# Soft-MoE combine weights laid out by PE and ACT, a second inner-layer buffer, dispatch maxima read from PSUM

## The chip, the cores and the metric

The kernel runs on one core of a Trainium2 chip. The metric is the device time of one execution in microseconds (us), as the median of several runs. Engines are named as the profiler names them: PE (matrix products; PEld is its weight load), DVE (VectorE), ACT (ScalarE), POOL (GpSimd) and SP, which here issues DMA transfers. Each engine executes its own instructions in program order and waits on semaphores for the others.

## What is computed

Three layers follow one another. Pooled attention has 8 batches of 8 heads with 576 queries of width 64, and keys and values averaged over groups of 8. Its 4608 output rows of width 512 are the tokens x of a soft mixture of experts, with 8 experts of 4 slots each. Then comes a two-layer network of inner width 2048.

```python
# attention, per batch and head
attn = softmax(q @ mean8(k).T / 8)
x = (attn @ mean8(v))              # -> 4608 x 512
# soft mixture of experts
logits = x @ phi                   # 4608 x 32
d = softmax(logits, axis=0)        # dispatch, over the tokens
slot_input = (d.T @ x).reshape(8, 4, 512)
for e in range(8):
    h = np.maximum(slot_input[e] @ w1[e], 0.0)   # 512 x 1024
    slot_out[e] = h @ w2[e]                      # 1024 x 512
c = softmax(logits, axis=1)        # combine, over the 32 slots
y = c @ slot_out.reshape(32, 512)
# network
r = np.maximum(y @ w_in, 0.0)      # 512 x 2048
out = (s * (r * r) + b) @ w_out    # 2048 x 512
```

## The kernel before

**Attention and dispatch.** A hand-written order of steps (the tables `LOOP` and `FIRST`) goes over the batches, two batches to a pair `pr`, and over their token tiles of 128. PE's short products share a ring of four PSUM banks (tile name `w`, handed out by `bank()`). When a batch's logits are there, its dispatch runs as a generator whose `yield`s are slots of the loop: column maxima (L546, L555), spread to all partitions by a product (L558), copied out of PSUM into `m_all` (L559, DVE), subtracted from the logits (L562, DVE), exponential (L564, ACT), then products of the result with the attention weights (L586, L591). Each batch uses its own maxima, and at the end the eight are brought to one scale (L524 to L534), which needs the copies in `m_all`.

**Experts.** The 8 MB of `w1` and as many of `w2` arrive in 32 transfers of 1 MB in the order of the list `EORD`, numbered n0 to n31 here. Experts 0 to 3 are group 0, experts 4 to 7 group 1. n0 to n7 are group 0's `w1`, n8 and n9 the first two of group 1's, n10 to n15 the first six of group 0's `w2`, n16 to n21 the other six of group 1's `w1`, n22 and n23 the last of group 0's `w2`, n24 to n31 all of group 1's. For a `w1` key PE runs four products (L969) into two PSUM tiles `l1[g]`, for a `w2` key four products (L977) into `so_ps`. The profile counts each of these as two matmuls. When a group's `w1` keys are done, `hidden(g)` copies the two PSUM tiles to `si_all` (L946 on ACT, L947 on DVE), turns them round by products with a selector (`hps`, L951) and writes the relu of that into `h1z` (L953, ACT), a zero-filled buffer with four columns per expert from which the `w2` products read their stationary operand. There is one `h1z`, for both groups. Loads come by SP's queue: `done(key)`, behind a key's products in the program, gives the slot back, and `pump()` puts the next load (L140) into SP's queue, where it waits for those products.

**Between the keys.** `BEHIND` says after which key which side work is started. `step_convs()` moves generators on that rewrite the network's weights to rounded high and low parts (L829 to L843 on DVE, ACT and POOL). Their DVE steps, ten at a time, stand in DVE's queue in front of L947.

**Combine weights.** The combine softmax (L748 to L758) leaves its weights in `L_all`, tokens on the partitions, 4 batch pairs of 32 slots beside one another, 9 token tiles per pair. The network's first product needs `cT`: slots on the partitions, tokens along the row, the rounded value (hi) in the 32-row blocks 0 and 2 and the remainder (lo) in blocks 1 and 3. `combine_t`, begun behind n15, transposes nine tiles on PE (L926), rounds them on ACT back into `L_all` (L927), forms the remainder on DVE in `kept[3]` (L929), a weight slot that is free by then, and then has SP move the bytes with 16 transfers of 32 partitions, 144 KB each (L935), into the four blocks of `cT`, pair after pair. SP's queue issues in program order, so the loads of the network's weights that come after stand behind these 16.

**Hand-over.** After n31 two products (L1004) on the `cT` data fill time on PE, `so_ps` is copied (L1008), turned round by products (L1011), copied (L1014), multiplied with `w_in` (L862, L868, L879, L884) to the matrix `S`, and `st_h` takes `S` with `cT` to the network's inner layer (L1050), of which relu, square and rounding follow (L1054 to L1079). The products L1106 with `w_out` then fill PE to the end.

## Time and profile before

| what | us |
|---|---|
| median of 3 runs (lowest, highest) | 693.62 (692.23, 693.72) |
| the profiled execution's own time | 692.57 |
| its span, first to last instruction | 690.8 |
| PE busy | 649.7 (94%) |
| DVE busy | 475.8 (69%) |
| ACT busy | 399.9 (58%) |
| POOL busy | 287.1 (42%) |
| matmuls of L1106 | 659.9 (225.2 + 224.9 + 209.8) |

The profile is of one execution; its times are from the start of the span. The three groups of L1106 overlap one another in PE's pipeline, so their sum is more than the time they take. The page's share of PE is a mean over stages with different limits. The stages, as the trace has them: attention to 203.2, the experts to 245.4, the hand-over to 251.6, the network from there to about 683, and the last output transfers. A view by windows gives the busy time of each engine in a stretch, and the granted clock of PE (1.00 is 2.4 GHz, 0.5 is 1.2 GHz). The timeline of an engine lists its instructions in order, runs of the same instruction put together (xcount), with the idle time in front and what ended it. The chain goes back from the last instruction to what released each step. An instruction of SP with a `DMA_DIRECT2D` is an issue; its landing is much later.

### The profile page before, as it was taken

Reading aid. Unit: us, or ns where it says so; the run is one execution under the profiler, and the core shown is the slowest. Engines: PE = TensorE matmul, PEld = TensorE weight load, DVE = VectorE, ACT = ScalarE, POOL = GpSimd, SP = SyncE. Lnnn points to the kernel's source line nnn. Section 1 sums busy time; section 2 is a strip of 40 time slices with the busy share of each in tenths; the row PEclk is TensorE's granted clock in tenths of the full one; section 3 lists DMA queues with packets and bytes.
Section 4 is the critical chain, followed back from the end, with each engine's and each line's share of the span. In section 5 each row is a group of like instructions: output and inputs, shape, how many; then the busy total and the mean of one; then the engine's idle time right before and its main releaser. Section 6 shows DMA issues by size and latency. Waiting matters only on the chain.

```text
span 690.8 us, 11197 instructions
## 1 busy us (share of the span) xinstructions
PE 649.7 (94%) x4307; PEld 520.0 (75%) x4307; DVE 475.8 (69%) x748; ACT 399.9 (58%) x659; POOL 287.1 (42%) x220
## 2 busy tenths in 40 slices
PE   7877989799989889999999999999999999999996
PEld 6665777678653358888888888888888888888885
DVE  6879778767663947887677778887556764566443
ACT  3565667566421267886666666666666666555551
POOL 3766466522100443563223434443232241899200
PEclk9998999999679899999999999999999999999999
DMA  8999486607599992011110110301100000222222
GB/s 287 399 340 288 154 245 245 218 29 258 185 362 374 366 277 82 1 61 62 61 62 1 61 62 1 121 14 49 61 1 1 0 1 0 93 93 92 92 92 91
DMA packets 42085, 91.23 MB, mean 132 GB/s; under 512 B 7216, under 2 KB 15408, under 8 KB 42032
## 3 DMA queue, kind: packets, MB, share of 16 engines
q1 hardware_dynamic: 42032, 90.52, 38.4%
q8 instruction: 34, 0.56, 0.3%
q14 instruction: 19, 0.16, 0.1%
HBM read 78.71 MB, written 9.44 MB: 128 GB/s over the span
## 4 chain that ended last, share of the span: by engine, by line
PE 78%; DVE 11%; DMA 4%; ACT 3%; SPq 1%; issue 1%; POOL 0%; DVEq 0%; ACTq 0%
PE o L1106 57%; PE h L1050 5%; PE sc L392 3%; DMA x<-in_moe_w_dram 2%; PE l L969 2%; DVE S L401 2%; DVE mx L399 2%; DVE sm L410 2%; PE w L443 1%; DMA ring<-in_q_dram 1%; PE w L609 1%; ACT S L409 1%; PE w L362 1%; PE w L586 1%; PE w L466 1%
## 5 line engine op out<-in xcount | busy, mean ns | idle before, releaser
L1106 PE MATMUL o<-whi,gh 128*128 128x512 f32 x576 | 225.2, 391 | 1.2 <-ACT gh L1076 1.2
L1106 PE MATMUL o<-wlo,gh 128*128 128x512 f32 x576 | 224.9, 390 | 0.0
L1106 PE MATMUL o<-whi,gl 128*128 128x512 f32 x576 | 209.8, 391 | 0.0
L1079 DVE TENSOR_TENSOR gl<-r,gh 128x768 fp32r<-128x768 f32 (+1 forms) x97 | 104.8, 1081 | 116.4 <-ACT gh L1067 116.1
L1059 ACT ACTIVATE r<-h 128x768 f32<-128x768 f32 x95 | 77.5, 816 | 142.2 <-PE h L1050 140.3
L1106 PEld LDWEIGHTS o<-whi,gl 128*128 128x128 f32 x576 | 108.2, 188 | 22.8
L1106 PEld LDWEIGHTS o<-whi,gh 128*128 128x128 f32 x576 | 108.1, 188 | 21.5 <-ACT gh L1076 1.5
L1106 PEld LDWEIGHTS o<-wlo,gh 128*128 128x128 f32 x576 | 108.2, 188 | 18.9
L842 POOL TENSOR_TENSOR fr<-fr,xp 128x512 f32<-128x512 f32 x28 | 45.2, 1613 | 173.9 <-ACT fr L841 156.7
L1119 DVE SCALAR_TENSOR_TENSOR part<-o,sb_t,part 128x512 f32<-128x512 f32 x144 | 96.9, 742 | 3.2 <-PE o L1106 3.1
L1060 ACT ACTIVATE r<-r 128x768 f32<-128x768 f32 x95 | 80.5, 848 | 3.0
L1067 ACT CAST gh<-r 128x768 fp32r<-128x768 f32 x95 | 79.4, 835 | 2.6
L430 POOL TENSOR_TENSOR P<-S,rs 128x576 f32<-128x576 f32 x32 | 37.3, 1166 | 74.1 <-DVE rs L413 39.1
L1216 POOL TENSOR_TENSOR part<-part,wsum 128x512 f32<-128x512 f32 x36 | 53.3, 1518 | 15.1 <-ACT wsum L1210 15.1
L1050 PE MATMUL h<-cT,S 128*128 128x384 f32 x192 | 49.3, 338 | 0.5 <-DVE S L885 0.5
L1050 PEld LDWEIGHTS h<-cT,S 128*128 128x128 f32 x192 | 36.0, 188 | 8.7 <-DVE S L885 0.7
L410 DVE TENSOR_REDUCE sm<-S 128x8 f32<-128x584 f32 x36 | 27.3, 758 | 20.5 <-ACT S L409 20.4
L392 PE MATMUL sc<-kb,qT 128*128 128x144 f32 x256 | 40.5, 305 | 0.2 <-ACT qT L364 0.2
L399 DVE TENSOR_REDUCE mx<-sc 128x8 f32<-128x576 f32 x36 | 26.4, 733 | 15.6 <-PE sc L392 13.1
L392 PEld LDWEIGHTS sc<-kb,qT 128*128 128x128 f32 x256 | 36.4, 206 | 0.7 <-ACT qT L364 0.5
L409 ACT ACTIVATE S<-S 128x576 f32<-128x576 f32 x36 | 24.6, 682 | 19.4 <-DVE S L401 19.1
L364 ACT COPY qT<-w 128x512 f32<-128x512 f32 x36 | 20.9, 584 | 21.6 <-PE w L362 20.9
(236 smaller groups left out, 884.6 us busy)
## 6 DMA issues: line engine op xcount, KB each, us to landing
x<-in_moe_w_dram SPq DMA_DIRECT2D x15, 1024.0 KB, 9.7
ring<-in_moe_w_dram SPq DMA_DIRECT2D x12, 1024.0 KB, 6.4
raw<-in_moe_w_in_dram SPq DMA_DIRECT2D x8, 1024.0 KB, 5.7
raw<-in_moe_w_out_dram SPq DMA_DIRECT2D x8, 1024.0 KB, 4.8
out_dram<-part SPq DMA_DIRECT2D x32, 256.0 KB, 2.7
ring<-in_q_dram SPq DMA_DIRECT2D x7, 1024.0 KB, 10.8
ring<-in_v_dram SPq DMA_DIRECT2D x9, 768.0 KB, 10.5
ring<-in_k_dram SPq DMA_DIRECT2D x7, 768.0 KB, 8.1
```

The source lines that it names most:

```text
L392: nc.tensor.matmul(out=sc[:, i // 2, 2 * KP * (i % 2):2 * KP * (i % 2) + 2 * KP], lhsT=qT[:, i, :], rhs=kb[:, H * bb + 4 * (j % 2) + i, :] ...
L399: nc.vector.tensor_reduce(out=mx, in_=scv, axis=AX.X, op=ALU.max)
L410: nc.vector.tensor_reduce(out=sm, in_=S, axis=AX.X, op=ALU.add)
L842: nc.gpsimd.tensor_tensor(out=fr, in0=fr, in1=xp, op=ALU.mult)
L1050: nc.tensor.matmul(out=h[x][:, 0:384] if i == 0 else h[:, x, 0:384], lhsT=Sw[:, f, :], rhs=cT(c, 384), start=True, stop=True)
L1059: nc.scalar.activation(out=r, in_=h[:, :, 0:384], func=ACTF.Relu)
L1060: nc.scalar.activation(out=r, in_=r, func=ACTF.Square)
L1067: nc.scalar.copy(out=gh_t[i], in_=r)
L1079: nc.vector.tensor_tensor(out=gl[:, x], in0=r[:, x], in1=gh[:, x].bitcast(F32), op=ALU.subtract)
L1106: nc.tensor.matmul(out=o_t[tt], lhsT=l[:, x, 128 * c:128 * c + 128], rhs=r, start=(fi == 0 and n == 0), stop=(fi == GROUPS[g] - 1 and n == 1),
L1119: nc.vector.scalar_tensor_tensor(out=p, in0=o_t[tt], scalar=sb_t[:, 0:1], in1=p, op0=ALU.mult, op1=ALU.add)
L1216: nc.gpsimd.tensor_tensor(out=p, in0=p, in1=wsum, op=ALU.add)
```

## The change

Three things change.

1. `combine_t` with its transfers goes. In its place `combine_hl(pr)`, one for each pair, forms hi (ACT) and lo (DVE) from the softmax while the tokens are still on the partitions, and puts them side by side, 32 columns each, into `kept[3]`. `combine_t(g)`, six times, transposes three pieces of 128 columns on PE, each with the hi and lo of two token tiles, into one PSUM tile `ct` (two buffers), and ACT copies it into `cT` with four copies of 64 partitions and 384 elements. The new `BEHIND` starts the four `combine_hl` behind n9 to n11 and the six `combine_t` behind n11 to n16. There are 18 transposes for 9, 24 ACT copies and 5 roundings for 3, 5 subtractions for 3, and no transfers for 16.
2. A second `h1z` takes `kept[3]` when the combine is done with it, zeroed on POOL behind n17 (`HZ`). `hidden(1)` writes into it, and its second copy runs on ACT instead of DVE.
3. In the dispatch, the subtraction reads the maxima from PSUM, in the slot where the copy stood; the exponential moves one slot up, and the copy into `m_all` comes after it, one slot later than before.

```diff
--- before.py
+++ after.py
@@ -20,7 +20,8 @@
 WIPOS, WOPOS = 25, 26
 
 
-BEHIND = {15: "c", 18: "i0", 19: "i1", 23: "o0", 24: "o1"}
+HZ = 17
+BEHIND = {9: "c0 c1", 10: "c2", 11: "t0 c3", 12: "t1", 13: "t2", 14: "t3", 15: "t4", 16: "t5", 18: "i0", 19: "i1", 23: "o0", 24: "o1"}
 TAIL = "F0 6 C4 X0 D2 6 X1 E2 6 m 6 6 F2 D3 m D4 6 E4 6 m F4 X2 7 W3 7 W2 7 7 7 M2 6 7 7 M3 6 7 M4 7"
 BUSY = (2, 0)
 CUT = 1
@@ -556,12 +557,12 @@
         yield
         ps = bank()
         nc.tensor.matmul(out=ps[:, 0:32], lhsT=mc.to_broadcast([32, 128]), rhs=ident[0:32, 0:32], start=True, stop=True)
+        dd = ap2.tile([128, 5, 32], F32, tag="dd", name="dd")
+        nc.vector.tensor_tensor(out=dd, in0=Lb, in1=ps[:, 0:32].unsqueeze(1).to_broadcast([128, 5, 32]), op=ALU.subtract)
+        yield
+        nc.scalar.activation(out=dd, in_=dd, func=ACTF.Exp)
         nc.vector.tensor_copy(out=m_all[:, b_, :], in_=ps[:, 0:32])
         yield
-        dd = ap2.tile([128, 5, 32], F32, tag="dd", name="dd")
-        nc.vector.tensor_tensor(out=dd, in0=Lb, in1=m_all[:, b_, :].unsqueeze(1).to_broadcast([128, 5, 32]), op=ALU.subtract)
-        yield
-        nc.scalar.activation(out=dd, in_=dd, func=ACTF.Exp)
         yield
         zd = ap2.tile([128, 32], F32, tag="zd", name="zd")
 
@@ -914,29 +915,34 @@
             convs.append(todo.popleft())
             next(convs[-1])
 
-    def combine_t():
-
-
-        x0 = 0
-        for j0, n in ((0, 4), (4, 4), (8, 1)):
-            x = 128 * n
-            Lc = L_all[:, 1 + j0:1 + j0 + n].rearrange("p j r s -> p (j r s)")
-            ps = ps_x.tile([128, 512], F32, tag="sx", name="ct")
-            for i in range(n):
-                nc.tensor.transpose(out=ps[:, 128 * i:128 * i + 128], in_=Lc[:, 128 * i:128 * i + 128], identity=ident)
-            nc.scalar.copy(out=Lc.bitcast(F32R), in_=ps[:, 0:x])
-            yield
-            nc.vector.tensor_tensor(out=kept[3][:, x0:x0 + x].bitcast(F32R), in0=ps[:, 0:x], in1=Lc, op=ALU.subtract)
-            x0 += x
-        hl = (L_all[:, 1:10].rearrange("p j r s -> p (j r s)"), kept[3][:, 0:x0])
-        for pr in range(NPR):
-            dst = cT(9 * pr * 128, x0).bitcast(F32)
-            for r in range(4):
-                nc.sync.dma_start(out=dst[32 * r:32 * r + 32], in_=hl[r % 2][32 * pr:32 * pr + 32])
+    def combine_hl(pr):
+
+        Lc = L_t[pr][:, 1:10, :]
+        hl = kept[3].rearrange("p (j z s) -> p j z s", z=2, s=32)
+        t0, t1 = 9 * pr, 9 * pr + 9
+        for a, e, o in ((t0, min(t1, 32), t0), (32, t1, 0)):
+            if a < e:
+                z = hl[:, o:o + e - a]
+                x = Lc[:, a - t0:e - t0]
+                nc.scalar.copy(out=z[:, :, 0].bitcast(F32R), in_=x)
+                nc.vector.tensor_tensor(out=z[:, :, 1].bitcast(F32R), in0=x, in1=z[:, :, 0], op=ALU.subtract)
+        yield
+
+    def combine_t(g):
+
+        ps = ps_x.tile([128, 3, 128], F32, tag="sx", name="ct")
+        hl = kept[3].rearrange("p (j x) -> p j x", x=128)
+        for i in range(3):
+            nc.tensor.transpose(out=ps[:, i], in_=hl[:, (3 * g + i) % 16], identity=ident)
+        dst = cT(768 * g, 768).rearrange("p (m a x) -> p m a x", m=3, a=2)
+        for j in range(2):
+            for r in range(2):
+                nc.scalar.copy(out=dst[64 * r:64 * r + 64, :, j], in_=ps[64 * j:64 * j + 64])
+        yield
 
     so_ps = ps_1.tile([128, 512], F32, tag="so", name="so_ps")
 
-    h1z = None
+    h1z = []
     wo_ = [conv_wo(f) for f in range(GROUPS[0])]
     todo.extend(cmb)
     l1 = [[ps_l.tile([128, 512], F32, tag="l1", name="l1") for _ in range(2)] for g in range(2)]
@@ -944,14 +950,14 @@
 
     def hidden(g):
         nc.scalar.copy(out=hs[:, 0:512], in_=l1[g][0])
-        nc.vector.tensor_copy(out=hs[:, 512:1024], in_=l1[g][1])
+        (nc.scalar.copy if g else nc.vector.tensor_copy)(out=hs[:, 512:1024], in_=l1[g][1])
         yield
         hps = ps_1.tile([128, 8, 32], F32, tag="hps", name="hps")
         for fc in range(8):
             nc.tensor.matmul(out=hps[:, fc, :], lhsT=hs[:, 128 * fc:128 * fc + 128], rhs=sel4, start=True, stop=True)
         yield
         nc.scalar.activation(
-            out=h1z.rearrange("p f (e r) -> p f e r", r=36)[:, :, :, 16:20],
+            out=h1z[g].rearrange("p f (e r) -> p f e r", r=36)[:, :, :, 16:20],
             in_=hps[:, :, 4 * EG * g:4 * EG * g + 4 * EG].rearrange("p f (e j) -> p f e j", j=4),
             func=ACTF.Relu,
         )
@@ -976,7 +982,7 @@
             for c in range(4):
                 nc.tensor.matmul(
                     out=so_ps[32 * c:32 * c + 32, :],
-                    lhsT=h1z[:, 4 * hf + c, 36 * ge + 16 - 4 * e:36 * ge + 48 - 4 * e],
+                    lhsT=h1z[g][:, 4 * hf + c, 36 * ge + 16 - 4 * e:36 * ge + 48 - 4 * e],
                     rhs=w[:, c, :],
                     start=(e == 0 and hf == 0), stop=(e == E - 1 and hf == 1),
                 )
@@ -984,16 +990,19 @@
         if n_ == BRIEF:
             brctx.close()
             cT_t.append(ctx.enter_context(tc.tile_pool(name="cv1", bufs=1, side="right")).tile([128, NTH], F32R, name="cT1"))
-        if h1z is None and kept:
-            h1z = kept[0][:, 0:1152].rearrange("p (f r) -> p f r", f=8)
-            nc.gpsimd.memset(h1z, 0.0)
+        if not h1z and kept or n_ == HZ:
+            h1z.append(kept[3 if h1z else 0][:, 0:1152].rearrange("p (f r) -> p f r", f=8))
+            nc.gpsimd.memset(h1z[-1], 0.0)
         advance(hid)
         if key == W1[g][-1]:
             hid.append(hidden(g))
             advance(hid)
-        if n_ in BEHIND:
-            x, f = BEHIND[n_][0], int(BEHIND[n_][1:] or 0)
-            todo.appendleft(conv_wi(f) if x == "i" else islice(wo_[f], 2) if x == "o" else combine_t())
+        for x in BEHIND.get(n_, "").split():
+            f = int(x[1:])
+            if x[0] in "ct":
+                next((combine_hl if x[0] == "c" else combine_t)(f))
+            else:
+                todo.appendleft(conv_wi(f) if x[0] == "i" else islice(wo_[f], 2))
         if key != EORD[-1]:
             step_convs()
     assert not todo, len(todo)
```

PE around the keys n10 to n17, the experts' stage. `so_ps` rows are `w2` keys (n10 to n15), `l_` rows `w1` keys, `ct` the transposes; before:

```order
L977 MATMUL so_ps<-raw_66,ring_76 32x512 x4
L977 MATMUL so_ps<-x,ring_76 32x512 x12
L977 MATMUL so_ps<-ring_81,ring_76 32x512 x4
L977 MATMUL so_ps<-x,ring_76 32x512 x4
L926 MATMUL ct<-ident,L 128x128 x4
L969 MATMUL l_2647<-x,siz 32x512 x2
L969 MATMUL l_2648<-x,siz 32x512 x2
L926 MATMUL ct<-ident,L 128x128 x4
L969 MATMUL l_2647<-x,siz 32x512 x2
L969 MATMUL l_2648<-x,siz 32x512 x2
L926 MATMUL ct<-ident,L 128x128
```

and with the change:

```order
L936 MATMUL ct<-ident,ring_79 128x128 x3
L983 MATMUL so_ps<-x,ring_76 32x512 x4
L936 MATMUL ct<-ident,ring_79 128x128 x3
L983 MATMUL so_ps<-x,ring_76 32x512 x4
L936 MATMUL ct<-ident,ring_79 128x128 x3
L983 MATMUL so_ps<-ring_81,ring_76 32x512 x4
L936 MATMUL ct<-ident,ring_79 128x128 x3
L983 MATMUL so_ps<-x,ring_76 32x512 x4
L936 MATMUL ct<-ident,ring_79 128x128 x3
L975 MATMUL l_2647<-x,siz 32x512 x2
L975 MATMUL l_2648<-x,siz 32x512 x2
L936 MATMUL ct<-ident,ring_79 128x128 x3
```

Three transposes now stand behind each key from n11 to n16, where before all nine stood behind n15, n16 and n17 (before, the row of 12 is three keys).

ACT from `hidden(0)` to `hidden(1)`, in the same stage: L946 and L953 are its copy and relu, L927 the rounding, L841 a conversion of network weights; before:

```order
L946 COPY si_all<-l_2645 128x512
L953 ACTIVATE ring_76<-hps 128x32x4
L927 CAST L<-ct 128x512 x2
L927 CAST L<-ct 128x128
L841 ACTIVATE ring_78<-raw_65 128x512 x2
L946 COPY si_all<-l_2647 128x512
L953 ACTIVATE ring_76<-hps 128x32x4
```

and with the change, where every line number is six higher from `hidden` on and L940 is the copy into `cT`:

```order
L952 COPY si_all<-l_2645 128x512
L959 ACTIVATE ring_76<-hps 128x32x4
L927 CAST ring_79<-L 128x9x32 x3
L940 CAST cT_2629<-ct 64x3x128 x4
L927 CAST ring_79<-L 128x5x32
L927 CAST ring_79<-L 128x4x32
L940 CAST cT_2629<-ct 64x3x128 x8
L940 CAST cT_2704<-ct 64x3x128 x12
L842 ACTIVATE ring_78<-raw_65 128x512 x2
L952 COPY si_all<-l_2647 128x512
L953 COPY si_all<-l_2648 128x512
L959 ACTIVATE ring_79<-hps 128x32x4
```

The 24 copies and the roundings now stand between the two `hidden`s, in front of the conversion and of the two copies L952 and L953.

SP's queue at the end of the experts: `x` is an expert weight slot, `raw_` a slot for raw network weights; before, with the first 2 of the 16 transfers and the last:

```order
L140 DMA ring_81<-in_moe_w_dram 128x4x512
L140 DMA x<-in_moe_w_dram 128x4x512 x2
L935 DMA cT_2629<-L 32x1152
L935 DMA cT_2629<-ring_79 32x1152
...
L935 DMA cT_2704<-ring_79 32x1152
L140 DMA raw_65<-in_moe_w_in_dram 128x4x512
L140 DMA raw_67<-in_moe_w_in_dram 128x4x512
L140 DMA raw_66<-in_moe_w_out_dram 128x2x1024
```

and with the change:

```order
L141 DMA ring_81<-in_moe_w_dram 128x4x512
L141 DMA x<-in_moe_w_dram 128x4x512 x2
L141 DMA raw_65<-in_moe_w_in_dram 128x4x512
L141 DMA raw_67<-in_moe_w_in_dram 128x4x512
L141 DMA raw_66<-in_moe_w_out_dram 128x2x1024
```

The raw loads now follow directly on the last two expert weights.

## Rows read from the trace of the kernel before

**Rows 1.** Windows: busy us (instructions) by engine, granted clock, DMA share, GB/s.

```profile
core 0: us, PE busy (x) PEld busy (x) DVE busy (x) ACT busy (x) POOL busy (x), PEclk, DMA share, GB/s
...
221.00:229.40 8.40, 8.40 (x73) 2.50 (x66) 5.24 (x10) 3.23 (x6) 1.06 (x1) 1.00 1.04 392
229.40:237.40 8.00, 4.88 (x32) 2.97 (x28) 7.76 (x11) 0.35 (x2) 4.13 (x4) 0.67 1.04 386
237.40:245.40 8.00, 7.77 (x64) 1.93 (x64) 4.14 (x5) 1.17 (x3) 5.17 (x4) 0.91 1.03 266
245.40:251.60 6.20, 3.93 (x35) 2.84 (x35) 1.92 (x6) 3.83 (x11) 1.26 (x1) 1.00 0.88 194
```

**Rows 2.** Chain that ended last: start us, us, what.

```profile
221.62 0.59 PE ct L926 x4
...
227.28 16.13 DMA x<-in_moe_w_dram
...
247.31 2.66 DMA cT<-L
```

**Rows 3.** Timeline of PE: start us, us, operation, [idle before <-releaser].

```profile
228.43 1.04 PE L977 MATMUL so_ps<-ring,ring 128*32 128x512 f32 x8
...
233.14 1.92 PE L951 MATMUL hps<-sel,si_all 128*128 128x32 f32 x8 [2.66 <-DVE si_all L947]
234.99 1.94 PE L977 MATMUL so_ps<-ring,ring 128*32 128x512 f32 x8
237.38 1.78 PE L977 MATMUL so_ps<-ring,ring 128*32 128x512 f32 x8 [0.46 <-ACT ring L953]
...
243.28 1.89 PE L977 MATMUL so_ps<-x,ring 128*32 128x512 f32 x16
245.42 0.74 PE L1004 MATMUL l<-cT 128*128 128x512 f32 x2 [0.25 <-DMA cT<-ring]
...
249.48 0.97 PE L1050 MATMUL h<-cT,S 128*128 128x384 f32 x4 [0.46 <-DVE S L885]
```

**Rows 4.** Timeline of DVE, same columns.

```profile
228.48 1.41 DVE L830 TENSOR_SCALAR ring<-ring 128x512 f32<-128x512 f32 x1
...
232.40 0.68 DVE L947 COPY si_all<-l 128x512 f32<-128x512 f32 x1
```

**Rows 5.** Timeline of SP's DMA issues.

```profile
224.28 5.54 SPq L140 DMA_DIRECT2D x<-in_moe_w_dram  x2
229.92 2.53 SPq L935 DMA_DIRECT2D cT<-L  x1
...
249.92 1.23 SPq L140 DMA_DIRECT2D raw<-in_moe_w_in_dram  x2
```

**Rows 6.** DMA view of L140: landings of the issues at 224.28 and 227.28.

```profile
DMA to landing us min/median/max: 14.5/15.3/16.1
```

**Rows 7.** DMA view, 236 to 240 and 240 to 243.4.

```profile
DMA packets 753, 1.55 MB, mean 386 GB/s; under 512 B 32, under 2 KB 32, under 8 KB 753
...
DMA packets 232, 0.68 MB, mean 199 GB/s; under 512 B 69, under 2 KB 69, under 8 KB 232
```

**Rows 8.** Groups of ACT copies by form: busy us, mean ns, idle.

```profile
L282 ACT ACTIVATE kb<-w 64x384 f32<-64x384 f32 x24 | 11.6, 485 | 9.6 <-PE w L275 9.3
...
L323 ACT COPY vpt<-w 64x288 f32<-64x288 f32 x8 | 2.7, 392 | 2.0 <-PE w L316 2.0
```

**Rows 9.** Timeline of ACT, one pair of copies.

```profile
69.03 0.69 ACT L323 COPY vpt<-w 64x288 f32<-64x288 f32 x2
```

**Rows 10.** Timeline of PEld at the last key.

```profile
243.71 0.12 PEld L977 LDWEIGHTS so_ps<-x,ring 128*32 128x32 f32 x4 [0.31 <-DMA x<-in_moe_w_dram]
```

**Rows 11.** Timeline of DVE at the last dispatch.

```profile
195.16 0.19 DVE L559 COPY m_all<-w 128x32 f32<-128x32 f32 x1 [0.50 <-PE w L558]
195.39 0.32 DVE L562 TENSOR_TENSOR dd<-L,m_all 128x160 f32<-128x160 f32 x1
```

**Rows 12.** Waits of PE, whole span: us in total, times, longest.

```profile
PE w L586 <- ACT dd L564: 1.0, 2, 0.8
```

## The prediction

> **What bounds the kernel now.** I read the windows by stage first, then the chain, and then engine by engine the one stage that the change touches. The MLP, from 251.60 us on, is out of reach: its matmuls follow one another without a gap that the change could close. What is left is the stretch between the end of attention (203.2) and the first MLP matmul (251.60): the experts, to 245.4, then the hand-over. In the windows [rows 1] PE is busy for only 4.88 of the 8.00 us from 229.4 to 237.4, at a mean clock of 0.67; from 237.4 to 245.4 it is nearly always busy and the rate of the DMA falls from 386 to 266 GB/s; in the hand-over, 245.4 to 251.6, PE is busy for 3.93 of 6.20.
>
> The printed chain [rows 2] goes through neither PE hole. It goes from the issue of the last expert weight (227.28) over its landing 16.13 us later (243.41), through SP's cT issues to a cT landing at 249.97. I believe its first half and not its second. The PE rows [rows 3] show why: the last two keys (`so_ps` matmuls) run at 243.28 to 245.2, as soon as that weight is there; L1004 then follows at 245.42 with 0.25 us of wait for a cT transfer, and from there a chain of small steps (the `so` copy that began at 245.30, L1011, L862, L868, L879, L884, L1050) reaches L1050 at 249.48. L1050's first half ends at about 249.96, which by itself explains when ACT's relu can start. So **the last weight's landing sets the end of the experts, and the small steps set the hand-over**; the cT transfers take part through what they do to that landing.
>
> PE was late as well. It stood 2.66 us before the second half of `hps`, because L947 on DVE stood behind ten conversion operations of 0.4 to 1.4 us each and ran only at 232.40 [rows 3, 4]. The next matmuls, 233.14 and 234.99, ran 1.92 and 1.94 us per 8, against 1.04 for 8 at 228.43: half clock. Then 0.46 us were lost before 237.38, since the relu into the one `h1z` waits for the readers of group 0. PE reached the last key at about 243.3 to 243.7. **Both limits meet within half a microsecond**, so removing only PE's or only the DMA's delay would give nothing. The change touches both, and the later of the two decides.
>
> **The DMA side.** All 16 cT issues go, 144 KB each: 2.36 MB. Before them the weights land in order and evenly: of the last two, the one issued at 224.28 takes 14.5 us (238.8), the one at 227.28 takes 16.1 (243.4) [rows 5, 6]. So the last one comes 4.6 us after its predecessor. At the steady rate of 386 GB/s 1 MB takes 1.049/0.386 = 2.7 us, and this rate is what holds to 240 [rows 7]. From 240 to 243.4 the same queue completes 232 packets at a mean rate of 199 GB/s. In the windows the engines are as busy as before there [rows 1]; the transfers into 32 partitions are mixed in. Without them the last weight lands at 238.8 + 2.7 = 241.5, **1.9 us earlier**. What now follows in the queue is 1 MB loads of the MLP's weights (before, from 249.92 on [rows 5]); loads of that kind followed one another through the whole stage at the steady rate, so they delay what is ahead of them little: 0 to 0.5 us. The issue of the last two weights must not become late. Their slots come free at keys that end at about 224 to 226 after the change too (below), and they queue for over 14 us, so a delay of 2 us on issue is covered.
>
> **The PE side, replayed.** To 216.3 nothing moves. Then six groups of three transposes stand between the keys n10 to n17, where before 4 + 4 + 1 stood at n15 to n17: nine more. Four take about 0.58 us of PE's time (0.59 in the chain [rows 2]), so nine cost 1.3. Each group is followed by four copies 64x384 out of PSUM on ACT, with two PSUM buffers. Their price has two bounds: 0.485 us each, as L282 (64x384) took [rows 8]; or less where copies overlap, as the 64x288 pair L323, where two of 0.392 took 0.69, so the second came 0.30 after the first [rows 8, 9]. Scaled to 384 elements, 0.30 gives 0.385 (an estimate). A group is then 0.385 x 4 + 0.1 = 1.65 us at the low price, 2.0 at the high one (0.485 x 4 + 0.1). PE has a key (0.97) and three transposes (0.45) per group, 1.4, so ACT paces it: PE waits from the third group on for a buffer. The low price gives about 0.3 to 0.45 at each of three groups, 1.0 in all; the high one about 2.2. I take the low one, since L323 is the same COPY out of 64 partitions of PSUM and L282 is an activation with a scale. The preparation (hi on ACT, the lo subtraction on DVE, for c0 to c3) runs beside the matmuls of n10, in a stretch where both engines waited; only the first group may wait for it, until about 218.0.
>
> So the group-1 keys of `w1`, which ended at 228.6, end at about 228.6 + 1.3 + 1.0 = 230.9 (between 230.2 and 232.1). n22 covers the first copy (L946, 0.59); the second, now on ACT too, ends at about 232.1, so the second half of `hps` starts there and not at 233.14. n23 and then n24 follow without the wait at 237.38, since the second `h1z` is zeroed at n17 and nothing reads it: `hps` ends at 233.1, n23 at 234.1. The holes that are left here are a few tenths each, as those of the hand-over are (0.25 before L1004, 0.46 before L1050 [rows 3]), where the clock stood at 1.00 [rows 1], so I reckon with full clock. Seven keys of 0.97, n24 to n30, end at 234.1 + 6.8 = **240.9**; at the dear copy price 242.1. Before, the half clock and the holes made it about 243.5.
>
> The later of 240.9 and 241.5 + 0.3 (the wait for the weight's load at 243.71 in front of the last key was 0.31 [rows 10]) is 241.8. From the landing to the end of the experts it was 243.4 to 245.2, 1.8, so the end is 243.3: **1.9 us earlier**. The hand-over has the same steps in the same order; L1004's 0.25 us of wait ran beside the `so` copy and gives nothing. The MLP begins 1.9 us earlier and is as long as before, because its weights now come earlier than they did.
>
> ACT's new work is 24 x 0.385 to 0.485, or 9 to 12 us, between 217 and 231; of the 8.4 us from 221 to 229.4 ACT was busy for 3.23 [rows 1]. It delays ACT's conversions (L841) by some five, and with them `ring` operations of DVE and POOL, whose users come in the MLP.
>
> For this choice of engine there is a contrary rule. The rows show 0.485 us for 384 elements on ACT and 0.68 us for DVE's copy of 512 [rows 4, 8]. The Trainium skill, "ScalarE: Activation LUTs", section "Rules for kernel authors", would rather have simple arithmetic on VectorE than on ScalarE. By that rule the six groups would have been split between two engines; here DVE had ten conversions queued at that place, so the sum would gain at most the 1.0 us of buffer waits, which the landing hides.
>
> **The dispatch.** The subtraction no longer waits for the copy of the maxima (0.19) and its gap: at the last batch 195.16 to 195.39, so 0.2 us earlier [rows 11]. In the loop PE waited 1.0 us in two places for that exponential [rows 12], of which half may go. Against it the PSUM bank is held one step longer, for all eight batches; the next users of the four banks can stop. At the batches where I could see a bank's next user close behind, that is 0.15 to 0.5 us each, three of them. Bounds: -1.0 and +1.5; I take -0.1, as both mostly fall beside PE's other work.
>
> **Sum.** 1.9 + 0.1 = 2.0. The profiled execution took 692.57 (span 690.8) and gives 690.6; the median of the runs is 693.62, 1.05 higher, which gives 691.6. I put the forecast between them, and count every case from 693.1: **691.1**.
>
> **The rivals.** *N, the landing stays.* If the last weight's slow stretch has another cause than the cT transfers (it is the last of its kind in the queue), it lands at 243.4 as before and only the dispatch's tenths are left: 692.9. For it: transfers behind another should not delay it, and PE's wait for that weight is but 0.31. Against it: the rate halves just where the cT transfers begin to follow [rows 7], and a single load has no other reason to. The Trainium skill, "DMA: Bandwidth & Descriptors", section "Queues, rings and completion order", says that within one queue of an engine descriptors are taken in ring order. By that alone the cT transfers would cost the weight nothing and the answer would be 692.9; the halved rate in the rows speaks against it, so I leave it 0.13.
>
> *P, ACT paces PE.* If the copies cost 0.485 and c0 to c3 come late, PE reaches the last key at 242.1 or, with waits at all six groups, at 243: the gain is 0.4 to 1.5, so 692.0 to 692.7. Chance 0.10.
>
> *E, both are earlier.* If the landing is at 240 or before and ACT's copies overlap, PE's chain sets the end, 240.9 + 1.0 against 245.2: 3.3, with 0.5 from the dispatch 689.3. Nothing shows a landing before 241, so 0.06.
>
> *T, the other side: half clock in the hand-over.* PE would come to the last key too early, stand for a microsecond or more for the weight, and go on at half clock. In the rows a hole of 2.66 us is followed by 1.92 and 1.94 per 8 matmuls instead of 1.04, and the clock was back only near 239 [rows 3]. The hand-over's PE work on the path is 3.93 - 0.74 (L1004, beside the copy) = 3.2 us [rows 1, 3]; at half clock it is 3.2 longer, against a gain of 2.0: +1.2, so 694.3. It decides if the hole before the last key comes near that one; my replay gives 0.9, and the smaller holes of the hand-over left the clock at 1.00 [rows 1]. Chance 0.09.
>
> *B, the banks.* The longer hold stops PE in attention by 1.5 more than it gains, or slightly above: 692.6 or more. Chance 0.07.
>
> **How the numbers follow.** The forecast has 0.55, N 0.13, P 0.10, E 0.06, T 0.09, B 0.07. A measurement of this kernel can tell about 0.2%, or 1.4 us, from no change. The forecast's gain, 2.0 with some 0.9 to either side, is over 1.4 three times in four: faster 0.41 and same 0.14. With E's 0.06, P and B a little, faster is 0.50; N, P and most of B give same 0.36; T and the rest of B slower 0.14. The range leaves out half of E and much of T: 689.4 to 693.9.
>
> **What would show it.** Right: no `hps` wait on a DVE copy; so_ps at 1.04 per 8 throughout; the last weight 2.7 us behind its predecessor; the experts' end at about 243.3 with the hand-over still 6.2 to 6.4 long. N shows as a spacing of 4.6 without any cT transfer; P as `ct` waits of PE on L940 of over 2 us; T as a clock of 0.5 in L1011 to L1050; B as new PE waits in attention whose releaser is the copy of the maxima.

## The result and the profile after

The changed kernel takes 686.32 us in the median (685.67 to 689.64, 5 executions), the kernel before 693.72 (692.23 to 695.21). The ratio is 0.9903, 95% interval [0.9873, 0.9932]: 6.7 us faster (4.7 to 8.8), against a forecast of 2.0. It lies below the range, which ended at 689.4. The profiled execution took 687.59, its span is 685.8 (before 690.8).

Windows of the changed kernel over the stretches of [rows 1] (columns as there):

```profile
core 0: us, PE busy (x) PEld busy (x) DVE busy (x) ACT busy (x) POOL busy (x), PEclk, DMA share, GB/s
221.00:229.40 8.40, 7.99 (x75) 3.65 (x71) 1.75 (x3) 6.74 (x14) 4.07 (x4) 1.00 1.05 387
229.40:237.40 8.00, 7.64 (x73) 2.11 (x72) 7.75 (x9) 1.58 (x3) 5.21 (x4) 1.00 1.05 386
237.40:245.40 8.00, 6.06 (x44) 4.07 (x37) 2.63 (x7) 4.73 (x12) 4.13 (x4) 0.80 0.66 252
```

From 229.4 to 237.4 PE is now busy for 7.64 us instead of 4.88, at clock 1.00 instead of 0.67, and the DMA keeps 386 GB/s to the last weight. But these windows lie at another place of the program than before: the stage has moved to the left. The timeline of PE (columns as in [rows 3]) shows by how much, first the row of before, then those of after (line numbers up to nine higher):

```profile
203.21 6.07 PE L969 MATMUL l<-ring,siz 128*32 128x512 f32 x32 [0.94 <-DVE siz L631]
```

```profile
197.42 5.54 PE L975 MATMUL l<-ring,siz 128*32 128x512 f32 x32 [0.94 <-DVE siz L632]
...
217.76 0.55 PE L936 MATMUL ct<-ident,ring 128*128 128x128 f32 x3 [0.58 <-ACT cT L940]
...
226.47 1.04 PE L983 MATMUL so_ps<-ring,ring 128*32 128x512 f32 x8
227.48 1.97 PE L957 MATMUL hps<-sel,si_all 128*128 128x32 f32 x16
229.38 1.92 PE L983 MATMUL so_ps<-ring,ring 128*32 128x512 f32 x16
...
236.81 1.07 PE L983 MATMUL so_ps<-x,ring 128*32 128x512 f32 x8 [0.36 <-DMA x<-in_moe_w_dram]
...
242.20 1.62 PE L1059 MATMUL h<-cT,S 128*128 128x384 f32 x4 [0.46 <-DVE S L886]
244.54 0.79 PE L1115 MATMUL o<-whi,gh 128*128 128x512 f32 x1 [0.72 <-ACT gh L1085]
```

The first expert product starts at 197.42; before, it started at 203.21. So **5.8 us are gained before the part of the program on which nearly all of the prediction is spent.** From there to the end of the last key it is 197.42 to 237.9, 40.5 us, against 203.21 to 245.2, 42.0: 1.5 gained. The hand-over takes 237.9 to 244.54, 6.7 against 6.4. The first products of the network then run at half clock to about 249 (0.79 and 0.63 each instead of 0.50 and 0.39), which gives back some 2 us in this execution. 5.8 + 1.5 - 0.3 - 2 is about the 5.0 by which the span shrank.

Where attention gained, two groups of each kernel show (group, busy us, mean ns, idle us before them with its releaser). Before:

```profile
L562 DVE TENSOR_TENSOR dd<-L,m_all 128x160 f32<-128x160 f32 x8 | 6.8, 853 | 0.0
...
L564 ACT ACTIVATE dd<-dd 128x160 f32<-128x160 f32 x8 | 2.7, 336 | 8.8 <-DVE dd L562 8.7
```

and after:

```profile
L561 DVE TENSOR_TENSOR dd<-L,w 128x160 f32<-128x160 f32 x8 | 2.5, 313 | 1.1 <-PE w L559 1.1
...
L563 ACT ACTIVATE dd<-dd 128x160 f32<-128x160 f32 x8 | 2.7, 338 | 2.8 <-DVE dd L561 2.8
```

The subtraction of the maxima took 853 ns in the mean of its eight instructions, and takes 313 now. ACT stood 8.8 us in front of the exponential, with the rest of its queue behind it, and stands 2.8 now. The prediction put no price on it: it counted the copy in front of it at the last batch, where the subtraction's row shows 0.32 us [rows 11]. What made the others slow stands in the timelines of DVE and POOL before, side by side:

```profile
69.50 1.61 DVE L562 TENSOR_TENSOR dd<-L,m_all 128x160 f32<-128x160 f32 x1
...
69.11 1.81 POOL L260 TENSOR_TENSOR ring<-ring 128x768 f32<-128x768 f32 x1
...
90.92 1.86 DVE L562 TENSOR_TENSOR dd<-L,m_all 128x160 f32<-128x160 f32 x1
...
90.80 1.80 POOL L260 TENSOR_TENSOR ring<-ring 128x768 f32<-128x768 f32 x1
```

Each slow subtraction begins just behind a POOL instruction that reads two operands from SBUF, and ends 0.2 us behind that instruction's end (71.11 against 70.92, 92.78 against 92.60; at 113.7 and 133.5 likewise, 1.03 and 1.05 us). With one of its two operands in PSUM it takes 0.31 in all eight batches. The Trainium skill, "SBUF — State Buffer", section "Who interferes with whom", states just this: a DVE instruction with two SBUF inputs contends with a GpSimd instruction that reads SBUF. It calls the port pair that the two share an exclusive lock, and says that a DVE instruction with at most one SBUF input, outside its two-port modes, doesn't contend. The rows agree with it: 1.03 to 1.86 us beside a POOL instruction with two inputs in SBUF, 0.31 with one in PSUM. It would have changed the sum, and the prediction didn't look for it.

### The profile page after: what moved, and what is told of

It reads as the page before. It is cut to its first block, busy times and chain, and to the rows that moved or that the text cites. A ratio compares the mean times of both kernels' runs of the same rounds, so it can differ in the third digit from the quotient of the medians.

```text
span 685.8 us, 11208 instructions
## 1 busy us (share of the span) xinstructions
PE 646.9 (94%) x4316; PEld 516.4 (75%) x4316; DVE 471.0 (69%) x749; ACT 412.6 (60%) x686; POOL 288.3 (42%) x221
## 4 chain that ended last, share of the span: by engine, by line
PE 79%; DVE 10%; DMA 5%; ACT 3%; issue 1%; SPq 1%; DVEq 0%; POOL 0%; ACTq 0%
PE o L1115 57%; PE h L1059 5%; PE sc L393 3%; DVE S L402 2%; DMA x<-in_moe_w_dram 2%; PE w L444 2%; DVE mx L400 1%; DVE sm L411 1%; PE w L363 1%; DMA ring<-in_q_dram 1%; PE w L610 1%; ACT S L410 1%; DMA brief<-in_moe_w_dram 1%; PE w L587 1%; PE w L467 1%
## 5 line engine op out<-in xcount | busy, mean ns | idle before, releaser
L1059 PE MATMUL h<-cT,S 128*128 128x384 f32 x192 | 49.9, 342 | 0.5 <-DVE S L886 0.5
L1059 PEld LDWEIGHTS h<-cT,S 128*128 128x128 f32 x192 | 36.4, 190 | 8.7 <-DVE S L886 0.7
L393 PE MATMUL sc<-kb,qT 128*128 128x144 f32 x256 | 39.0, 297 | 0.2 <-ACT qT L365 0.2
L393 PEld LDWEIGHTS sc<-kb,qT 128*128 128x128 f32 x256 | 35.0, 199 | 0.7 <-ACT qT L365 0.5
```

The costliest lines, as they stand in the source:

```text
L393: nc.tensor.matmul(out=sc[:, i // 2, 2 * KP * (i % 2):2 * KP * (i % 2) + 2 * KP], lhsT=qT[:, i, :], rhs=kb[:, H * bb + 4 * (j % 2) + i, :] ...
L1059: nc.tensor.matmul(out=h[x][:, 0:384] if i == 0 else h[:, x, 0:384], lhsT=Sw[:, f, :], rhs=cT(c, 384), start=True, stop=True)
```

## The experiments

Profiles of one kernel differ by where PE falls to half clock, and times of one kernel's executions by up to 9 us. So each verdict rests on the ratio, and the trace is used for what doesn't hang on the clock.

**The dispatch alone**: the kernel before with the one hunk of the diff that stands in the dispatch.

```diff
+        dd = ap2.tile([128, 5, 32], F32, tag="dd", name="dd")
+        nc.vector.tensor_tensor(out=dd, in0=Lb, in1=ps[:, 0:32].unsqueeze(1).to_broadcast([128, 5, 32]), op=ALU.subtract)
+        yield
+        nc.scalar.activation(out=dd, in_=dd, func=ACTF.Exp)
         nc.vector.tensor_copy(out=m_all[:, b_, :], in_=ps[:, 0:32])
         yield
-        dd = ap2.tile([128, 5, 32], F32, tag="dd", name="dd")
-        nc.vector.tensor_tensor(out=dd, in0=Lb, in1=m_all[:, b_, :]...
-        yield
-        nc.scalar.activation(out=dd, in_=dd, func=ACTF.Exp)
         yield
```

> The kernel before with the third part of the change alone (the subtraction from PSUM one slot earlier, the copy one slot later). In the trace of after, attention ends 5.8 us earlier: 2.1 of it are there at 150 us, the other 3.7 arise between 177 and 195, where PE of before ran at half clock and PE of after did not. Theory D (the dispatch alone makes both): 4 to 6 us faster, about 688.5, and no half clock between 177 and 191. Theory D-: only the 2.1 us come from the dispatch, the clock stretch is a coin that falls anew in each execution: about 691.5. The prediction's own term: 0.1 faster, 693.6.

Ratio 0.9949 [0.9921, 0.9976]: 3.5 us faster (1.7 to 5.5). That lies between theory D and theory D-, and is 35 times the prediction's 0.1. The sign that D named did not come: in this profile the clock from 170 to 190 is 0.83, not 1.00 as in that of the changed kernel. The profile of this kernel also shows what the experts of before do with a gain that comes to them (PE timeline at the last key):

```profile
238.63 1.03 PE L977 MATMUL so_ps<-x,ring 128*32 128x512 f32 x8
241.91 1.07 PE L977 MATMUL so_ps<-x,ring 128*32 128x512 f32 x8 [2.25 <-DMA x<-in_moe_w_dram]
243.80 0.73 PE L1004 MATMUL l<-cT 128*128 128x512 f32 x2 [0.82 <-DMA cT<-ring]
```

PE reaches the last key early and stands 2.25 us for the last weight, then 0.82 more for a cT transfer: the weight still comes late behind its predecessor, and PE, earlier now, can't cover it.

**The rest alone**: the changed kernel with that hunk taken back.

> The changed kernel with the dispatch of before: only the combine by PE and ACT, no transfers, and the second h1z. The prediction's term for this part was 1.9 us: 691.8. If instead most of the measured 7.4 us comes from here (theory X), it is below 689. In its trace the attention part is the same code as before: if the half clock from 177 to 191 is there again, it belongs to that code and is no accident of one execution.

Ratio 0.9960 [0.9934, 0.9985]: 2.8 us faster (1.0 to 4.6), around the 1.9 of the prediction. In its profile the stage from the first expert product (201.70) to the last key's end (241.6) takes 39.9 us, 2.1 less than before, PE waits 0.67 us for the last weight, and L1059 runs at full clock:

```profile
240.49 1.07 PE L983 MATMUL so_ps<-x,ring 128*32 128x512 f32 x8 [0.67 <-DMA x<-in_moe_w_dram]
...
245.86 0.97 PE L1059 MATMUL h<-cT,S 128*128 128x384 f32 x4 [0.46 <-DVE S L886]
```

The two parts together, 0.9949 x 0.9960 = 0.9909, are the whole within the intervals.

**Slot or operand.** Two kernels split the dispatch edit. One moves the subtraction up and leaves both operands in SBUF:

```diff
         nc.vector.tensor_copy(out=m_all[:, b_, :], in_=ps[:, 0:32])
-        yield
         dd = ap2.tile([128, 5, 32], F32, tag="dd", name="dd")
         nc.vector.tensor_tensor(out=dd, in0=Lb, in1=m_all[:, b_, :]...
         yield
         nc.scalar.activation(out=dd, in_=dd, func=ACTF.Exp)
+        yield
```

> The kernel before, copy of the maxima where it was, and behind it in the same slot the subtraction from the copy; the exponential one slot earlier. So the slot moves and the operand does not (both operands in SBUF). Theory O (the operand: a subtraction of two SBUF operands stands while a POOL instruction runs, 1.0 to 1.9 us instead of 0.31 in four batches): the subtraction is still slow wherever POOL runs at its new place, so under 1 us of gain if POOL runs there, the whole 2 us if it does not. Theory S (the slot: only the earlier start matters): the same gain as the dispatch edit as a whole.

The other leaves the slot and changes the operand:

```diff
-        nc.vector.tensor_tensor(out=dd, in0=Lb, in1=m_all[:, b_, :]...
+        nc.vector.tensor_tensor(out=dd, in0=Lb, in1=ps[:, 0:32]...
```

> The kernel before with the copy and the subtraction in their old slots, the subtraction reading the maxima from PSUM. So the operand moves and the slot does not. Theory O: the subtraction takes 0.31 us in all eight batches instead of 0.32 to 1.86, and 1.5 to 2 us of the gain at 150 us are there. Theory S: the subtraction is faster, but the exponential still comes late, and less than 0.7 us of the gain is there.

Ratios 0.9941 [0.991, 0.9973] for the slot, 0.9971 [0.9944, 0.9998] for the operand; the two intervals overlap. The groups of the subtraction and of the exponential, first slot, then operand:

```profile
L561 DVE TENSOR_TENSOR dd<-L,m_all 128x160 f32<-128x160 f32 x8 | 5.5, 692 | 0.3
...
L563 ACT ACTIVATE dd<-dd 128x160 f32<-128x160 f32 x8 | 2.7, 338 | 3.2 <-DVE dd L561 3.1
```

```profile
L562 DVE TENSOR_TENSOR dd<-L,w 128x160 f32<-128x160 f32 x8 | 2.5, 312 | 0.0
...
L564 ACT ACTIVATE dd<-dd 128x160 f32<-128x160 f32 x8 | 2.7, 336 | 5.6 <-DVE dd L562 5.5
```

The stretch from the first L609 of batch 0 to that of batch 1, at full clock in all these profiles, is 19.88 us before (77.75 to 97.63), 18.66 with the slot, 18.62 with the operand and 18.48 after (L610, 77.23 to 95.71). So **in this stretch either half alone brings nearly all of the gain**: each theory got its own kernel right there and was wrong to rule out the other. Whether that holds for the whole time the ratios leave open. With the slot the subtraction is still slow (692 ns), but has a slot of time in hand; with the operand it is fast in the old slot. What cost time there was the exponential's lateness in ACT's queue, by the one exponential that lies in the stretch: ACT waits 1.87 us for its subtraction before and 0.32 with the operand, and with the slot (90.41) and after (87.58) it doesn't wait. First before, then operand:

```profile
92.82 0.34 ACT L564 ACTIVATE dd<-dd 128x160 f32<-128x160 f32 x1 [1.87 <-DVE dd L562]
```

```profile
90.95 0.34 ACT L564 ACTIVATE dd<-dd 128x160 f32<-128x160 f32 x1 [0.32 <-DVE dd L562]
```

That the operand escapes POOL is plain in the timelines of the second one, where the subtraction runs inside a POOL instruction and takes 0.31:

```profile
90.48 1.81 POOL L260 TENSOR_TENSOR ring<-ring 128x768 f32<-128x768 f32 x1
...
90.61 0.31 DVE L562 TENSOR_TENSOR dd<-L,w 128x160 f32<-128x160 f32 x1
```

**The landing of the last weight.** In the kernel before, `combine_t` starts behind n27 instead of n15.

```diff
-BEHIND = {15: "c", 18: "i0", 19: "i1", 23: "o0", 24: "o1"}
+BEHIND = {18: "i0", 19: "i1", 23: "o0", 24: "o1", 27: "c"}
```

> The kernel before with the start of the combine transposes moved from behind n15 to behind n27, so that SP issues three 1 MB loads of the network's weights behind the last expert weight and only then the 16 cT transfers. What is read is the landing of the last expert weight, not the time, which suffers because the network's first product then waits for cT (some 5 us slower than before). If the cT transfers slow the last weight (the prediction's step), it lands 2.6 to 2.9 us behind its predecessor. If it is slow for another reason, being the last (rival N), 4 us or more, as before.

The last two weights are issued at 225.13 and about 2.6 later, and take 14.0 and 14.1 us; the last one lands 2.6 us behind its predecessor, not 4.6 as before. The DMA view over the last one's stretch, and PE's row at the last key:

```profile
DMA packets 504, 1.00 MB, mean 386 GB/s; under 512 B 14, under 2 KB 14, under 8 KB 504
...
241.84 1.06 PE L977 MATMUL so_ps<-x,ring 128*32 128x512 f32 x8 [1.43 <-DMA x<-in_moe_w_dram]
```

386 GB/s, with 1 MB loads behind it in the queue; with cT transfers behind it, 199 [rows 7]. The other profiles say the same: issue and time to landing put the last weight 4.4 to 5.1 us behind its predecessor in all five with cT transfers behind it, and 2.6 to 3.3 us in all seven without. Rival N falls, and with it the time that the prediction worked out from the ring order. The Trainium skill, "DMA: Bandwidth & Descriptors", section "Queues, rings and completion order", speaks of the order in which descriptors are taken, which no run here shows; whatever it was, the transfers behind did slow the load ahead. (The time, 705.25 in one execution, is of no use: the network waits for cT.)

**PE's hole alone.** The kernel before with the second copy of `hidden(1)` on ACT.

```diff
-        nc.vector.tensor_copy(out=hs[:, 512:1024], in_=l1[g][1])
+        (nc.scalar.copy if g else nc.vector.tensor_copy)(out=hs[:, 512:1024], in_=l1[g][1])
```

> The kernel before with one thing of the second part alone: the second copy of group 1 on ACT instead of DVE. The prediction says that PE's delay and the last weight's landing meet within half a microsecond, so that removing PE's alone gives nothing: PE's hole of 2.66 us and the half clock behind it go, PE waits 2 us or more for the last weight instead, and the time is within 0.7 us of before. Theory X: PE's hole was the bound, and 2 us or more are gained.

Ratio 1.0027 [1.0004, 1.005]: 1.9 us **slower** (0.3 to 3.5). The hole of 2.66 in front of `hps` is gone, and PE's rows read:

```profile
227.98 1.97 PE L951 MATMUL hps<-sel,si_all 128*128 128x32 f32 x16
...
237.98 1.06 PE L977 MATMUL so_ps<-x,ring 128*32 128x512 f32 x8 [1.22 <-DMA x<-in_moe_w_dram]
242.38 1.35 PE L977 MATMUL so_ps<-x,ring 128*32 128x512 f32 x8 [3.34 <-DMA x<-in_moe_w_dram]
...
247.49 1.08 PE L862 MATMUL o<-ring,sot 128*32 128x128 f32 x16 [0.45 <-ACT sot L1014]
...
250.05 1.65 PE L1050 MATMUL h<-cT,S 128*128 128x384 f32 x4 [0.26 <-DVE S L885]
```

PE now stands 1.22 and 3.34 us for the last two weights, and the products behind that run at half clock (L862 1.08 instead of 0.65, L1050 1.65 instead of 0.97). That is rival T as it was drawn, with the wait that it needs. From the first expert product (201.85) to the last key's end this profile takes 41.9 us, as before (42.0), and the hand-over takes 8.7 instead of 6.4. So in this pair of profiles the experts gained nothing, and the loss is in the hand-over's clock. The DMA's half shortens the wait and doesn't rule the fall out: in the six profiles of the changed kernel and its variants PE waits for that weight 0, 0, 0.36, 0.67, 0.88 and 1.87 us, and the first products of the network run at half clock in three of them: at 0.36, at 1.87 and at 0 (the last one of the runs below).

**One buffer.** The changed kernel with a single `h1z`.

```diff
-        if not h1z and kept or n_ == HZ:
+        if not h1z and kept:
...
-            out=h1z[g].rearrange("p f (e r) -> p f e r", r=36)[:, :, :, 16:20],
+            out=h1z[0].rearrange("p f (e r) -> p f e r", r=36)[:, :, :, 16:20],
...
-                    lhsT=h1z[g][:, 4 * hf + c, 36 * ge + 16 - 4 * e:36 * ge + 48 - 4 * e],
+                    lhsT=h1z[0][:, 4 * hf + c, 36 * ge + 16 - 4 * e:36 * ge + 48 - 4 * e],
```

> The changed kernel without its second h1z buffer: the relu of group 1 waits again for the readers of group 0 and the last keys read the one buffer. Prediction's step: the second buffer saves a wait of 0.46 us of PE, and the last weight's landing decides, so within 0.7 us of the changed kernel. Theory C (the wait matters because PE's clock falls after it): 2 us or more slower, with half clock behind n23.

Ratio 0.9901 [0.9867, 0.9936] beside 0.9905 for the changed kernel on the same chip: no difference that can be measured. The wait is there (0.40 on ACT's relu) and the last weight hides it. In this profile too the hand-over fell to half clock behind a wait for the weight:

```profile
229.97 1.07 PE L983 MATMUL so_ps<-ring,ring 128*32 128x512 f32 x8 [0.40 <-ACT ring L959]
...
238.06 1.07 PE L983 MATMUL so_ps<-x,ring 128*32 128x512 f32 x8 [1.87 <-DMA x<-in_moe_w_dram]
...
243.74 1.65 PE L1059 MATMUL h<-cT,S 128*128 128x384 f32 x4 [0.26 <-DVE S L886]
```

**The changed kernel once more**, with no edit.

> The changed kernel once more, beside the others. Its ratio, measured 0.9903, against the sum of its two parts measured alone (0.9949 and 0.9960, together 0.9909). Additive parts: 0.988 to 0.993. If the dispatch's gain is lost in the experts of before, where the last weight then waits for the DMA (the profile of the dispatch alone shows PE waiting 2.25 us for it), the whole is more than the sum: below 0.989. In the profile, the clock from 170 to 200 and from 242 to 250 tells whether the half clock seen there belongs to the code.

Ratio 0.9905 [0.987, 0.994]: the first figure stands, and it is as near to the product of the parts as the intervals can tell. In this profile L1059 (243.60, 0.98) and what follows ran at full clock, so the half clock at the start of the network belongs to single executions. No wait stands in front of the last key here: PE, and not the weight, was the later of the two. From 170 to 190 the clock is 0.83 in this profile and 1.00 in the first, so that stretch too differs between executions of one kernel.

**Filling the hand-over.**

```diff
-OPS = "o0 a0 o0 a1 b0 b1 h0 g0 o1 h1 o1 g1"
+OPS = "o0 a0 o0 a1 b0 b1 h0 w2 g0 o1 h1 o1 g1"
-BUSY = (2, 0)
+BUSY = (2, 1)
```

> The changed kernel with three more filler products in the hand-over: one behind L1020 and two behind the first L1059. In the profile of the changed kernel PE runs at half clock from L1059 at 242.2 to about 249, some 2 us lost. If the holes of the hand-over bring that on (theory C), the filled version runs L1059 and the first L1115 at full clock and is 0.5 to 2 us faster in the median. If the fall has nothing to do with these holes, the same time, or 0.3 us slower for the added products.

Ratio 0.9896 [0.9861, 0.9932] against 0.9905: inconclusive. The hand-over was at clock 1.00 in this profile, but so it was in the unfilled one above.

**Filling the end of attention** (`W` and a number in `TAIL` are so many transposes of the identity).

```diff
-TAIL = "F0 6 C4 X0 D2 6 X1 E2 6 m 6 6 F2 D3 m D4 6 E4 6 m F4 X2 7 W3 7 W2 7 7 7 M2 6 7 7 M3 6 7 M4 7"
+TAIL = "F0 6 C4 X0 D2 W8 6 X1 E2 6 m 6 6 F2 D3 m D4 6 E4 6 m F4 X2 7 W3 7 W2 7 7 7 M2 6 7 7 M3 6 7 M4 W5 7 W5"
```

> The changed kernel with idle products of PE (transposes of the identity, 128x128) in three holes at the end of attention: eight in the hole of 1.6 us before L554, five in that of 0.92 before the last L620, five in that of 0.94 before the first expert product. In all profiles so far PE runs at half clock for one, two or three stretches of about 6.8 us between 170 and 210, and the times of one kernel's executions follow the mean clock. Theory C (these holes bring the stretches on): the clock is 1.00 to 210 and the time 2 to 4 us below the changed kernel, about 683 to 685. Theory C- (the stretches come from something else): no difference, or up to 1 us slower for the added products.

Ratio 0.9901 [0.9876, 0.9926], as the changed kernel. The clock rose as theory C says, up to a point (its mean over an execution is 0.985 to 0.988 in the six executions here, 0.975 to 0.985 in the eleven of the changed kernel), but its 2 to 4 us did not come: the time stayed. Windows (columns as in [rows 1]) of the kernel before, of the changed one and of this one:

```profile
170.00:190.00 20.00, 18.34 (x161) 14.14 (x162) 13.52 (x29) 8.78 (x24) 4.60 (x4) 0.69 0.50 173
190.00:210.00 20.00, 17.59 (x187) 10.36 (x179) 14.20 (x45) 4.70 (x13) 1.61 (x2) 0.80 0.97 358
```

```profile
170.00:190.00 20.00, 16.55 (x214) 11.95 (x216) 15.18 (x37) 9.17 (x27) 4.42 (x4) 1.00 0.71 253
190.00:210.00 20.00, 17.45 (x158) 9.18 (x156) 12.96 (x39) 3.65 (x9) 1.06 (x1) 0.83 1.02 374
```

```profile
170.00:190.00 20.00, 17.34 (x218) 13.10 (x210) 14.71 (x36) 8.23 (x24) 4.43 (x4) 1.00 0.71 253
...
190.00:196.80 6.80, 6.70 (x88) 6.04 (x81) 4.24 (x16) 1.18 (x4) 0.00 (x0) 1.00 1.01 406
...
203.50:210.50 7.00, 6.93 (x40) 1.62 (x40) 2.41 (x9) 0.46 (x2) 0.00 (x0) 0.57 1.04 388
...
203.56 1.94 PE L975 MATMUL l<-brief,siz 128*32 128x512 f32 x8 [3.13 <-DMA brief<-in_moe_w_dram]
```

Here PE is at full clock until it begins the experts at 196.79; then it stands 3.13 us for the weight in `brief`, and behind that its mean clock is 0.57. In this profile what the clock gives, the landing of that weight takes back (the first profile of the changed kernel waited 0.69 us for it, at 203.65, and the second not at all). No version of these beats the changed kernel by more than the intervals.

## Why the prediction was wrong

**The step that failed is the dispatch term.** "Bounds: -1.0 and +1.5; I take -0.1": measured alone it is 3.5 us (1.7 to 5.5), outside its own bounds. Three readings made it small. It counted the copy of the maxima and its gap, 0.2 us at the last batch [rows 11], and put the subtraction's own length at nothing gained: that batch's row has 0.32 us for it, where the group has a mean of 853 ns. It counted only PE's wait for the exponential, 1.0 us [rows 12], where ACT waited 8.8 us for the subtraction and what stands behind it in ACT's queue came late: at 72.45 PE waited 1.05 us for a copy that ACT runs behind the exponential, and that is 0.17 now (first before, then after):

```profile
72.45 0.49 PE L275 MATMUL w<-ident,kp 128*64 128x128 f32 x3 [1.05 <-ACT LT L478]
```

```profile
71.93 0.49 PE L276 MATMUL w<-ident,kp 128*64 128x128 f32 x3 [0.17 <-ACT LT L479]
```

And "both mostly fall beside PE's other work" was said without a row. In the profiles PE reaches the eight transposes of L305 (L306 after) at 150.57 to 151.08 with the old dispatch (four profiles) and at 147.58 to 149.84 with the new (six): 2.3 us between the means. Of these, 1.5 are there at full clock: from the first L609 of batch 0 (L610 after) to these transposes it is 72.9 to 73.0 us in the three profiles with the old dispatch and a clock of 1.00 from 80 to 150, and 71.4 to 71.5 in the six with the new. (With the operand alone it is 71.8; the profile of the slot alone, which reached the transposes only at 153.33, has a clock of 0.89 to 80 us and of 0.98 from there to 150 and can't be compared.) The first expert product comes at 201.12 to 203.21 with the old and at 196.79 to 200.35 with the new.

**What lies between these 2.3 us and the 5.8 of the two profiles** goes mostly with the clock at the end of attention. By the windows just shown, the profile of before lost (1 - 0.69) x 20 + (1 - 0.80) x 20 = 10.2 us' worth of clock between 170 and 210, that of after 3.4, and the second profile of the changed kernel 6.8; the profiles of the other kernels lie from 3.4 to 8.6. So a part of the 5.8 is the draw of these two executions. But not all of what the clock gives is a draw. Each execution's mean clock was measured: on the same chip it is 0.973 in the mean of the 12 executions with the dispatch alone and 0.969 in that of the 35 of before, with a scatter of 0.003 to 0.004 from one to the next. The difference, 0.0036, has a 95% interval of about 0.001 to 0.006. Among those 35 executions 0.01 of clock goes with 4.0 us, so 0.0036 is about 1.4 us (an estimate). With the 1.5 at full clock that makes 2.9 of the 3.5. The prediction had no term for the clock in the dispatch. In which stretch the new dispatch keeps it, and by which wait, no run shows.

**The experts' term, 1.9, holds**: 2.8 (1.0 to 4.6) by the ratio, 2.1 by the stage of that profile. That stage takes 41.9 to 44.2 us in the five profiles with cT transfers behind the last weight and 39.9 to 41.7 in five of the six of the changed kernel and its variants; in the sixth, which stood 3.13 us for `brief`, it takes 43.3. That the term holds is in part luck, as its steps show:

- The landing "2.7 us behind its predecessor": 2.6 in the kernel where it could be read alone.
- "the last weight's landing sets the end of the experts": not by the rows of before. The weight landed at 243.41. PE ran the last two keys without a gap [rows 3], and keys of that kind follow one another by 0.86 us there, so the last one began at about 244.1: PE was the later by some tenths. The 0.3 that the sum puts in as a wait for the weight [rows 10] stands in front of the loads of the keys before it too, as in this line of the same view, with no DMA behind it:

```profile
243.28 0.12 PEld L977 LDWEIGHTS so_ps<-x,ring 128*32 128x32 f32 x4 [0.31 <-issue]
```

- "From the landing to the end of the experts": 241.8 and 1.8 are 243.6, not 243.3. And the 1.8 of before holds some 0.7 us of the key in front; a last key alone takes 1.07. From 241.8 the end would be 242.9, or 2.3 us earlier. The slips partly cancel.
- "the later of the two decides": PE waits 0.36 us for the weight in one profile of the changed kernel and not at all in the other, so the two limits still meet. Of "removing only PE's or only the DMA's delay would give nothing" the first half is right, and more than that: PE's half alone is 1.9 us slower. The DMA's half was not timed alone.
- The copies into `cT`: the low price was taken, 0.385, and the dear one came true, as the timeline of ACT after shows (twenty copies in 9.74 us, 0.487 each):

```profile
213.28 1.93 ACT L940 CAST cT<-ct 64x384 fp32r<-64x384 f32 x4 [1.08 <-PE ct L936]
...
215.78 9.74 ACT L940 CAST cT<-ct 64x384 fp32r<-64x384 f32 x20
...
226.84 0.59 ACT L952 COPY si_all<-l 128x512 f32<-128x512 f32 x1
227.32 0.59 ACT L953 COPY si_all<-l 128x512 f32<-128x512 f32 x1
```

  PE waited for them 0.58, 0.42 and 0.41 us, 1.4 in all, between the 1.0 and the 2.2 of the two prices. An activation with a scale [rows 8] and these copies out of 64 partitions cost the same; the pair of L323 [rows 9], another shape, was the wrong row. From the first expert product to the last key PE then took 39.0 us (197.42 to 236.45), where the replay had 37.7 at the low price and 38.9 at the dear one. The landing hid it in that profile, by 0.36 us.
- The second `h1z`: "0.46 us", worth nothing while the landing decides; so it is.
- The hand-over "6.2 to 6.4 long": 6.7 in the profiled execution, by the half clock from L1059 on.

**The rivals.** N is refuted by the landing without cT behind it. T happened with one buffer and with PE's hole alone, behind waits of 1.87 and 3.34 us for the last weight. In the first profile of the changed kernel the clock fell from L1059 on behind a wait of only 0.36; in its second profile it did not, nor in two neighbours behind waits of 0.67 and 0.88, and in a third it fell just behind the hand-over without any such wait. So the length of that wait alone doesn't decide it, and what does is open. P's sign, `ct` waits of over 2 us, was not reached (1.4); its own gain of 0.4 to 1.5 is 691.6 to 692.7, not 692.0 to 692.7. E's 689.3 is the nearest to the measured time, but not by its mechanism: the copies did not overlap, and its gain was to come from the experts. B shows as waits of 0.16 and 0.17 us behind the copy of the maxima in two of the profiles, and nothing more.

**The range** was built from the experts' uncertainties with 0.5 us of gain from the dispatch at most (in E). Even the term's own bound, 1.0, was taken from PE's waits alone; ACT's wait of 8.8 us, the longest in the chain of the changed instructions, would have shown that more was possible. The intervals of the ratios here, some 2 us to either side, are also wider than the 1.4 us that the prediction gave a measurement.

## What to carry to other kernels

Price an operation by its group, the mean and the largest, not by the nearest single row; where the mean is far above the smallest, look at what ran on POOL in just those instances, before the edit is called free. For an edit on one engine's queue, read the waits of every engine that the instruction releases, not PE's alone. Where two limits meet within a microsecond, lift both in one edit: lifting one can cost time (here 1.9 us, 0.3 to 3.5), by the clock that PE loses while it waits for the other.

## What the runs showed of the hardware

- A DVE subtraction of 128x160 with both operands in SBUF took 0.98 to 1.88 us where a POOL instruction of two SBUF operands had begun before it, and 0.31 with one operand in PSUM, at the same place.
- 1 MB weight loads behind one another on SP's queue keep 386 GB/s; transfers from SBUF to SBUF into 32 partitions behind the last of them bring the rate to 199 GB/s while that load is still under way, and its landing from 2.6 us behind its predecessor (2.6 to 3.3 in seven profiles) to 4.6 (4.4 to 5.1 in five).
- Copies of 64x384 from PSUM to SBUF on ACT, with rounding, did not overlap: one every 0.487 us in a row of twenty.
